# The last two chunks of a maxout layer in seven block products in place of eight

## The chip, the core and the metric

The kernel runs on one core of a Trainium2 chip. A core has TensorE (PE in the profile; its weight loads are PEld), VectorE (DVE), ScalarE (ACT), GpSimd (POOL) and SyncE (SP), whose queue starts most transfers (DMA). The measure is the device time of one execution in microseconds (us), as a median of runs.

## What is computed

```python
scores = scale * np.matmul(q, k.transpose(0, 1, 3, 2))      # 8 batches, 8 heads, 576 tokens, 64 wide
scores = np.where(mask, scores, -1000000000.0)              # mask: causal by blocks of 64 tokens
scores = scores - np.max(scores, axis=-1, keepdims=True)
attn = np.exp(scores)
attn = attn / (np.sum(attn, axis=-1, keepdims=True) + 1e-09)
attn_out = np.matmul(attn, v)
x = np.ascontiguousarray(attn_out.transpose(0, 2, 1, 3)).reshape(B * S, H * D)   # 4608 x 512
h = np.maximum(np.maximum(x @ w1, x @ w2), x @ w3)          # 512 x 768 each
out = h @ w_out                                             # 768 x 512
```

All is 32-bit. The weights come as 64-bit numbers and are rounded in the kernel.

## The kernel before

**Attention.** A `Pair` is two heads of one batch (four pairs a batch). `qk` makes the scores, `least` the row minima on VectorE, `exp` the exponentials on ScalarE, `turn` transposes them on VectorE into `pz`, `move` reshuffles `pz` into `pt` by eight transfers on SyncE's queue, and `pv` multiplies by the values. The result `x` is transposed: 128 features (one pair) by 512 tokens. The last 64 of a batch's 576 tokens (`ov`) are written to a scratch tensor `over` in device memory (method `put` of `Pair`; its end is the job `spilt`). TensorE runs `pv` of one pair with `qk` of the next (`both`); the last pair of all runs it by itself (`alone`).

**The layer.** A `Chunk` is 512 tokens of one batch; the ninth, `b == B`, is the leftover tokens of all batches, fetched back from `over`. Each 32-bit operand is split into two parts that TensorE takes at full rate: a high part (a cast on ScalarE: `xh`, `hh`) and a low part, the rest (a subtraction of two SBUF tensors on GpSimd or VectorE: `xl`, `hl`). A product of 128x128 by 128x512 is then three matmuls: high by high, high by low, low by high. The first layer (`product`) takes, for each of 6 blocks of 128 hidden units, 3 weight matrices and 4 blocks of features, three matmuls: 216 of them, each 512 columns wide, per chunk. `most` takes the running maximum: the first matrix is copied from PSUM on ScalarE, the other two are maxima on VectorE. The second layer (`project`) is 72 matmuls: for each of 4 token tiles 6 blocks, with `hh` and `hl` made in two groups of three blocks. `get` copies the result on ScalarE into `osb`, and `put` writes it out.

**Order.** Every step is a `Job` with a cost per engine, a rank, the jobs it waits for and the buffers it takes. `in_order` is run when the program is built: it fixes which engine takes a job (of those named in its cost) and the order on each engine. The chip then follows that order, engine by engine, and waits by semaphores on the data alone. PSUM has eight banks, five named `sb` (attention) and three named `pm` (layer). Ranks come from tables written by hand (`UNITS`, `PAIRS`, `STARTS`). The weights are prepared in the first 180 us and stay in SBUF as high and low parts (`wh`, `wl`, `woh`, `wol`).

Of the kernel before, what the change touches and what calls it, by code (L numbers as in the profile page):

```python
# [161 lines left out]
def kernel(  # L162
# [317 lines left out]
    class Head:  # L480
# [139 lines left out]
        def exp(self, eng, t):  # L620
            (nm, sm, _), c = self.stat, COL[t]
            self.p[t] = att.tile([P, P * (t + 1)], F32, name=f"p{t}", bufs=slots[f"p{t}"])
# [39 lines left out]
    class Pair:  # L662
# [124 lines left out]
        def plan4(self, first, tq, last):  # L787
# [307 lines left out]
    class Chunk:  # L1095


        def __init__(self, b, pairs, prior, start, end):
# [4 lines left out]
            xjobs = []
            for c in range(NC):
                if full:
                    ready = [pairs[c].ready]
                else:
                    ready = [job({"SP": LOAD}, start - 4, self.fetch, c, after=[q[c].spilt for q in pairs], take=("x32",), lasts=LOAD + DMA)]
# [202 lines left out]
```

## Time and profile before

| | |
|---|---|
| median of 3 runs | 879.0 us (878.9 to 883.0) |
| the profiled execution's own time | 879.9 us |
| its span, first to last instruction | 878.1 us |
| TensorE busy | 856.4 us, 98% |
| VectorE, ScalarE, GpSimd busy | 575.3, 463.7, 207.4 us |
| granted clock of TensorE, mean | 0.997 |

Times in rows are us from the start of the span. A timeline row gives start, duration, engine, line, operation, output and inputs, and in brackets the idle time ahead of it and what ended it. The profiled execution's own time is 1.8 us more than its span and 0.9 us more than the median.

### The profile page before, as it was taken

The page shows a single profiled execution, that of the slowest core. Times are in us where ns is not written, and L with a number is a line of the kernel's source. Part 1 is how long each engine was busy: PE and PEld are TensorE (multiplying, and loading weights), DVE is VectorE, ACT ScalarE, POOL GpSimd, SP SyncE. Part 2 cuts the span into 40 slices and gives each one's busy share as a digit, 9 for nine tenths or more (in the row PEclk, how much of TensorE's full clock was granted, in tenths as well). Part 3 has the DMA queues.
Part 4 walks back from the last instruction along what each step waited for, and adds up shares of the span by engine and source line. Part 5 has one row for each costly group of instructions (what it writes and reads, how often), then busy time and mean ns, then how long its engine had stood idle before and what let it go on. Part 6 is the DMA issues. An engine that isn't in the chain of part 4 may idle for free.

```text
span 878.1 us, 14264 instructions
## 1 busy us (share of the span) xinstructions
PE 856.4 (98%) x4646; PEld 661.7 (75%) x4646; DVE 575.3 (66%) x1583; ACT 463.7 (53%) x1269; POOL 207.4 (24%) x196
## 2 busy tenths in 40 slices
PE   7989999999999999999999999999999999999997
PEld 5656676777777777777777777777777778888885
DVE  5999998987877676857777677667666662222211
ACT  5778666765656454755576455645574343112102
POOL 1112442522415122422232223222241210001000
PEclk9999999999999999999999999999999999999999
DMA  6964365576565655565456555655566305001002
GB/s 156 239 192 107 90 148 155 117 170 137 129 139 124 153 112 106 106 147 115 109 119 149 115 117 116 159 110 118 118 162 133 83 22 147 1 1 49 1 0 49
DMA packets 233738, 99.26 MB, mean 113 GB/s; under 512 B 189888, under 2 KB 227776, under 8 KB 233664
## 3 DMA queue, kind: packets, MB, share of 16 engines
q1 hardware_dynamic: 219392, 95.99, 47.3%
q10 hardware_dynamic: 14272, 2.36, 1.5%
q8 instruction: 37, 0.61, 0.3%
q14 instruction: 37, 0.30, 0.1%
HBM read 41.94 MB, written 10.49 MB: 60 GB/s over the span
## 4 chain that ended last, share of the span: by engine, by line
PE 79%; DVE 11%; DMA 3%; ACT 2%; SPq 2%; issue 1%; POOL 1%; DVEq 0%; ACTq 0%; POOLq 0%
PE pm L1198 47%; PE pm L1232 14%; PE sb L1070 8%; PE sb L980 6%; PE sb L996 3%; DVE sb L460 3%; DMA nat<-in_k_dram 1%; DVE wo L361 1%; DVE pz L646 1%; DMA pt<-pz 1%; ACT p L626 1%; DMA wo<-in_moe_w_out_dram 1%; DVE wo L348 1%; SPq L656 1%; PE sb L580 1%
## 5 line engine op out<-in xcount | busy, mean ns | idle before, releaser
L1198 PE MATMUL pm<-xh,w 128*128 128x512 f32 x1296 | 424.4, 397 | 0.0
L1198 PEld LDWEIGHTS pm<-xh,w 128*128 128x128 f32 x1296 | 243.3, 188 | 55.3 <-issue 1.3
L1198 PE MATMUL pm<-xl,w 128*128 128x512 f32 x648 | 253.1, 391 | 0.5 <-POOL xl L273 0.5
L460 DVE CUSTOM_DVE_ANT_0 sb<-sb,mask 128x512 f32<-128x512 f32 (+3 forms) x288 | 144.8, 528 | 68.8 <-PE sb L980 42.7
L626 ACT ACTIVATE p<-sb,nm 128x256 f32<-128x256 f32 (+3 forms) x256 | 133.9, 530 | 63.7 <-DVE nm L460 60.0
L646 DVE STREAM_TRANSPOSE pz<-p 128x512 f32<-128x512 f32 (+1 forms) x280 | 137.9, 529 | 22.7 <-ACT p L476 18.0
L1198 PEld LDWEIGHTS pm<-xl,w 128*128 128x128 f32 x648 | 121.9, 188 | 25.2 <-POOL xl L273 0.9
L1211 DVE TENSOR_TENSOR m<-pm,m 128x512 f32<-128x512 f32 x108 | 73.3, 678 | 98.4 <-PE pm L1198 97.6
L1232 PE MATMUL pm<-wo,hh 128*128 128x512 f32 x432 | 135.2, 394 | 0.4 <-ACT hh L268 0.4
L478 POOL TENSOR_TENSOR p<-p,rs 128x128 f32<-128x128 f32 (+3 forms) x91 | 66.6, 754 | 236.6 <-DVE rs L785 220.4
L1070 PE MATMUL sb<-pt,vn 128*64 128x320 f32 (+2 forms) x840 | 90.7, 361 | 4.6 <-ACT p L626 2.1
L1232 PEld LDWEIGHTS pm<-wo,hh 128*128 128x128 f32 x432 | 79.9, 188 | 18.3 <-ACT hh L268 0.8
L268 ACT COPY m<-pm 128x512 f32<-128x512 f32 x54 | 31.6, 585 | 112.7 <-PE pm L1198 112.7
L1070 PEld LDWEIGHTS sb<-pt,vn 128*64 128x64 f32 x840 | 56.1, 137 | 42.4 <-issue 12.9
L1232 PE MATMUL pm<-wo,hl 128*128 128x512 f32 x216 | 84.4, 391 | 0.0
L980 PE MATMUL sb<-kq 64*128 64x512 f32 (+3 forms) x704 | 81.1, 354 | 1.9 <-ACT kq L268 0.5
L980 PEld LDWEIGHTS sb<-kq 64*128 64x128 f32 x704 | 58.1, 185 | 29.1 <-issue 13.7
L476 ACT ACTIVATE p<-p,rs 128x256 f32<-128x256 f32 (+3 forms) x133 | 66.8, 553 | 23.6 <-DVE rs L785 23.5
L273 POOL TENSOR_TENSOR kq<-nat,kq 128x1152 fp32r<-128x1152 f32 x21 | 56.4, 2684 | 71.8 <-ACT kq L268 39.8
L268 ACT CAST hh<-m 128x384 fp32r<-128x384 f32 x72 | 35.3, 514 | 49.6 <-PE pm L1232 28.0
L273 DVE TENSOR_TENSOR hl<-m,hh 128x384 fp32r<-128x384 f32 x54 | 39.3, 729 | 32.7 <-ACT hh L268 32.4
L273 POOL TENSOR_TENSOR xl<-x,xh 128x512 fp32r<-128x512 f32 x26 | 34.0, 1314 | 97.0 <-ACT xh L268 76.5
(105 smaller groups left out, 811.6 us busy)
## 6 DMA issues: line engine op xcount, KB each, us to landing
pt<-pz SPq DMA_DIRECT2D x224, 200.0 KB, 3.9
w<-in_moe_w_dram SPq DMA_DIRECT2D x18, 512.0 KB, 5.4
vn<-in_v_dram SPq DMA_DIRECT2D x64, 128.0 KB, 2.5
out_dram<-osb SPq DMA_DIRECT2D x32, 256.0 KB, 2.8
nat<-in_k_dram SPq DMA_DIRECT2D x112, 72.0 KB, 2.4
nat<-in_q_dram SPq DMA_DIRECT2D x96, 72.0 KB, 2.8
wo<-in_moe_w_out_dram SPq DMA_DIRECT2D x6, 512.0 KB, 5.9
nat<-in_q_dram ACTq DMA_DIRECT2D x16, 72.0 KB, 3.3
```

Of the source, the lines that this page charges most:

```text
L268: nc.scalar.copy(dst, src)
L273: {"DVE": nc.vector, "POOL": nc.gpsimd}[eng].tensor_tensor(out=dst, in0=a, in1=b, op=ALU.subtract)
L460: nc.vector.tensor_tensor_reduce(out=ps, in0=ps, in1=hidden, scale=-SCALE, scalar=first, op0=ALU.add, op1=ALU.min, accum_out=out_)
L476: nc.scalar.mul(p, p, r)
L478: nc.gpsimd.tensor_tensor(out=p, in0=p, in1=r.broadcast_to([P, p.shape[1]]), op=ALU.mult)
L626: nc.scalar.activation(dst, src, AF.Exp, bias=nm[:, c : c + 1], scale=-1.0, accum_out=sm[:, c : c + 1])
L646: nc.vector.transpose(dst, p[:, 0 : n * P])
L980: nc.tensor.matmul(ps, self.q[a][h.own, P * t : P * (t + 1)], self.k[b][h.own, 0:w], start=(a, b) == turns[0], stop=(a, b) == turns[-1],)
L1070: nc.tensor.matmul(o[h.own].rearrange("p (i u) -> p i u", u=n)[:, :, c0 : c0 + z - a], self.vn[:, kt, h.j, :], h.pt[:, :, a:z], start=(m = ...
L1198: nc.tensor.matmul(self.ps, w[i, f][:, c, :], xx, start=(c == 0 and s == 0), stop=(c == NC - 1 and s == 2))
L1211: nc.vector.tensor_tensor(out=m, in0=ps, in1=m, op=ALU.max)
L1232: nc.tensor.matmul(self.po, h, w[f], start=(f == 0 and s == 0), stop=(f == NF - 1 and s == 2))
```

## The change

The last batch's chunk and the chunk of leftovers, 1,024 tokens together, are taken as one by a new class `Double`. Its first layer is a 2x2 block product: two hidden blocks (`fp` numbers the three pairs of them) by two halves of the features on the weights' side, two halves of the features by two chunks on the data's side. Strassen's algorithm in Winograd's form makes it from seven block products, `P1` to `P7`, of 6 matmuls each. There are 9 such sets (3 pairs of blocks, 3 matrices), numbered `n`. For each set the sums of weight blocks `S1` to `S4` are made anew: two additions that put high and low part together (512 wide), four block sums, and four splits into high and low (all 256 wide). The sums of data blocks `T1` to `T4` are made once, in place, before the first set; the leftovers are fetched for that into buffers of the attention that have come free (`nat`, `vn`, `p4`). The results are put together from PSUM with temporaries `t0`, `t1`, `t2` (`p1`, `U2`, `p5`, `U3`, `C11` to `C22`), and `M12`, `M21`, `M22` are the running maxima. In a set, `P2` is added to `P1`'s bank and `P3` to `P5`'s, after a copy of each on ScalarE. The second layer follows for all 8 token tiles. The attention's and the weights' tables are changed too.

```diff
+    LAST = 2
...
-    UNITS = (0, 0, -1, 0, -4, 1, 0, 4, 9, 2, -8, 2, 2, 7, -3, -2, -2, -2, 0, -3, -2, -7, -5, -7)
-    PAIRS = (-1, 17, 1, 0, 4, 0, 0, -1, -8, -13, -15, -23)
-    STARTS = (0, 1, -2, -2, -2, -3, -2, -21, -1, -4, -1)
+    UNITS = (0, 0, -1, 0, -4, 1, 0, 0, 9, 2, -8, 2, 1, 7, -3, -2, -2, -1, 0, -6, -3, -7, -7, -9)
+    PAIRS = (-1, 17, 1, 0, 4, 0, 0, -1, -8, -13, -15, -23, 0, 2, -4, -1, 0, 0, 0, 0, 0, 0, 0, 0, 0, -4, -2, -2, -6, -8, -4, -6)
+    STARTS = (7, 2, -2, -2, -2, -3, -3, -22, -4, -5, 3)
...
+    SEVEN = {
+        "P1": ("A11", "B11", "a"),
+        "P2": ("A12", "B21", "a"),
+        "P3": ("S4", "B22", "c"),
+        "P4": ("A22", "T4", "e"),
+        "P5": ("S1", "T1", "c"),
+        "P6": ("S2", "T2", "b"),
+        "P7": ("S3", "T3", "d"),
+    }
+    FIRST_SEVEN = ("P1", "P5", "P2", "P6", "P7", "P3", "P4")
+    NEXT_SEVEN = ("P1", "P6", "P2", "P5", "P7", "P3", "P4")
...
+    class Double:
...
+            for c in range(2):
...
+                    for k, hp in (("x1", c), ("x3", c + 2))
+                )
+                b11, b21 = (pairs[c + n].ready for n in (0, 2))
...
+                l11 = parts("B11", "x0", b11)
+                t1 = sub("x1", "x0", "x0", l11, b12)
+                l1 = parts("T1", "x0", t1)
+                l22 = parts("B22", "x3", b22)
+                t3 = sub("x3", "x1", "x1", t1, b22)
+                l3 = parts("T3", "x1", t3)
+                t2 = sub("x3", "x0", "x0", l1, b22)
+                l2 = parts("T2", "x0", t2)
+                l21 = parts("B21", "x2", b21)
+                t4 = sub("x0", "x2", "x2", t2, l21)
+                l4 = parts("T4", "x2", t4)
...
+            hold = job({"SP": 1.0}, start, lambda eng: None, after=(prior.projected,), take=("hi", "hi"))
...
+            fresh = dict.fromkeys(("S1", "S2"), [hold]) | dict.fromkeys(("S3", "S4"), [last.last4, *free["p2"]])
...
+            for fp in range(3):
+                for i in range(3):
+                    left = self.lefts(n, fp, i, start + step * 7 * n, [*split, *(gone if n == 3 else ())], fresh)
+                    split = [left[x][0] for x in left]
+                    done, ranks = {}, {}
+                    for k, name in enumerate(NEXT_SEVEN if n else FIRST_SEVEN):
+                        a, b, bank = SEVEN[name]
+                        first = name in ("P1", "P6", "P5", "P7", "P4")
+                        after = [chain, ops[b, 0], ops[b, 1], prior.projected]
...
+                        chain = done[name] = job(
+                            {"PE": 6 * pe(N)}, start + step * (7 * n + k), self.product, n, fp, i, name, after=after, take=(TAGS[bank],) if first else ()
+                        )
...
+                        vec, both, m0 = {"DVE": dve(N) + 5.0}, two(N), i == 0
+                        if name == "P1":
+                            ev("p1", {"ACT": act(N)}, chain, ends.get("t0"), gate)
+                        if name == "P6":
+                            ev("U2", vec, chain, done["p1"], give=("sb",))
...
+                            ev("U3", vec, chain, done["U2"], ends.get("t1"), gate, give=("sb",))
+                            ev("C22", both, done["U3"], done["p5"])
...
+                        if name == "P3":
+                            ev("C12", vec, chain, done["U2"], done["U3"], give=("sb",))
...
+                        if name == "P4":
+                            ev("C21", vec, chain, done["C22"], give=("pm",))
...
+        def lefts(self, n, fp, i, rank, free, fresh):
+            two = lambda n: {"POOL": pool(n), "DVE": dve(n) + 5.0}
+            r = rank - 12
+            w = [
+                job(two(512), r, self.whole, n, fp, i, j, after=[units[i, 2 * fp + j].done, *free], ports=True) for j in range(2)
...
+            s1 = job(two(256), r, self.part, n, "S1", after=w[1:], ports=True)
+            s3 = job(two(256), r, self.part, n, "S3", after=[*w, s1], ports=True)
+            s2 = job(two(256), r, self.part, n, "S2", after=[s1, s3], ports=True)
+            s4 = job(two(256), r, self.part, n, "S4", after=[s2], ports=True)
+            out_ = {}
+            for name, after in (("S2", [s2, s4]), ("S1", [s1, s2]), ("S3", [s3]), ("S4", [s4])):
+                h = job({"ACT": act(256, False)}, r, self.high_s, n, name, after=[*after, *fresh[name]])
+                out_[name] = [job(two(256), r, self.low_s, n, name, after=(h,), ports=True)]
...
+        def product(self, eng, n, fp, i, name):
+            a, b, bank = SEVEN[name]
+            first = name not in ("P2", "P3")
+            if first:
+                pool_ = psm if TAGS[bank] == "pm" else psa
+                self.ps[bank] = pool_.tile([P, N], F32, name=TAGS[bank])
+                self.ps[n, bank] = self.ps[bank]
+            ps = self.ps[n, bank]
+            ah, al = self.left(n, fp, i, a)
+            for c in range(2):
+                bh, bl = (self.op(b, c, low) for low in (0, 1))
+                for s, (w, xx) in enumerate(((ah, bh), (ah, bl), (al, bh))):
+                    nc.tensor.matmul(ps, w[:, c, :], xx, start=(first and c == 0 and s == 0), stop=(c == 1 and s == 2), **({} if first else dict(skip_group_check=True)))
...
-    made[-1].alone(rank + SECOND)
+    made[-1].alone(rank + LAST)
...
-    for b in range(B + 1):
-        prior = Chunk(b, pairs[b] if b < B else pairs, prior, starts[b], starts[b + 1])
+    for b in range(B - 1):
+        prior = Chunk(b, pairs[b], prior, starts[b], starts[b + 1])
+    Double(pairs[B - 1], pairs, prior, starts[B - 1], starts[B + 1])
```

How the order moves, at three places. First TensorE at the last attention output (`L1070` and `L1072` are `pv`, `L1232` and `L1226` the second layer of batch 6's chunk, `L1198` a product of the last batch's chunk). Before:

```order
L1232 MATMUL pm<-wo_1815,hh 128x512 x2
L1232 MATMUL pm<-wo_1815,hl 128x512
L1198 MATMUL pm<-xh_7811,w_340 128x512
L1198 MATMUL pm<-xl_7819,w_340 128x512
L1198 MATMUL pm<-xh_7811,w_340 128x512
L1070 MATMUL sb<-pt,vn_103 64x320 x6
L1070 MATMUL sb<-pt,vn_103 64x4x48 x2
L1070 MATMUL sb<-pt,vn_103 64x4x16 x2
L1070 MATMUL sb<-pt,vn_103 64x256 x2
L1070 MATMUL sb<-pt,vn_103 64x4x32 x2
L1198 MATMUL pm<-xh_7814,w_340 128x512
```

TensorE after the change, at the same `pv`:

```order
L1226 MATMUL pm<-wo_1601,hh 128x512 x2
L1226 MATMUL pm<-wo_1601,hl 128x512
L1072 MATMUL sb<-pt,vn_103 64x320 x6
L1072 MATMUL sb<-pt,vn_103 64x4x48 x2
L1072 MATMUL sb<-pt,vn_103 64x4x16 x2
L1226 MATMUL pm<-wo_1618,hh 128x512 x2
L1226 MATMUL pm<-wo_1618,hl 128x512
...
L1226 MATMUL pm<-wo_1601,hl 128x512
L1072 MATMUL sb<-pt,vn_103 64x256 x2
L1072 MATMUL sb<-pt,vn_103 64x4x32 x2
L1226 MATMUL pm<-wo_1618,hh 128x512 x2
```

The `pv` now comes after 9 matmuls of the second layer and not after all 72, and its two halves stand apart, with 18 matmuls between them; 45 follow the second half, then the first `P1`.

Second, SyncE's queue at the last moves (`L656` and `L657` are `move`, `L1245` and `L1237` write results out, `L1187` and `L1414` fetch leftovers, `L897` and `L899` write them to scratch). Before:

```order
L1187 DMA x_7901<-over_116 128x512
L656 DMA pt<-pz 128x1x400 x4
L1245 DMA out_dram<-osb 128x512
L656 DMA pt<-pz 128x1x400 x4
L1245 DMA out_dram<-osb 128x512 x2
L897 DMA over_117<-ov 128x64
L1187 DMA x_8021<-over_117 128x512
```

SyncE's queue after the change:

```order
L899 DMA over_116<-ov 128x64
L657 DMA pt<-pz 128x1x400 x8
L1414 DMA nat<-over_116 128x512
L899 DMA over_117<-ov 128x64
L1237 DMA out_dram<-osb 128x512
L1414 DMA p_7937<-over_117 128x512
L1237 DMA out_dram<-osb 128x512 x3
```

All eight moves now stand together, with no write of results between them, and the fetches of the last leftovers go to `nat` and to `p4`'s buffer.

Third, ScalarE where batch 6's second layer ends and the last chunk's first layer begins (`osb` is `get`; `hh` is a high part). Before:

```order
L268 CAST hh<-m 128x384
L268 COPY osb<-pm 128x512
L268 COPY m<-pm 128x512
L268 COPY osb<-pm 128x512
L268 COPY m<-pm 128x512 x2
L268 CAST hh<-m 128x384 x3
```

ScalarE after the change, at the same end of batch 6's second layer (`p_8048` and `xh_8054` are high parts of `T3` and `T2`, `p_8016` of `S3`, the next `hh` of `S1`, `vn_103` is the copy of `P1`, then `hh` of `S2` and `q8r` of `S4`):

```order
L269 CAST hh<-m 128x384
L269 CAST pz<-x_7776 128x512
L269 COPY osb<-pm 128x512 x2
L269 CAST p_8048<-vn_102 128x512
L269 CAST xh_8054<-x_7533 128x512
L269 CAST p_8016<-m 128x256
L269 CAST hh<-m 128x256
L269 COPY vn_103<-pm 128x512
L269 CAST hh<-m 128x256
L269 CAST q8r_100<-m 128x256
```

Behind the last copy of the second layer ScalarE now has four high parts to make before `P1`'s copy; before, only a copy of the next chunk's first product stood there.

## Rows read from the trace of the kernel before

**Rows 1.** The page: busy time of TensorE, and the ending chain by line.
```profile
PE 856.4 (98%) x4646; PEld 661.7 (75%) x4646; DVE 575.3 (66%) x1583; ACT 463.7 (53%) x1269; POOL 207.4 (24%) x196
...
PE pm L1198 47%; PE pm L1232 14%; PE sb L1070 8%; PE sb L980 6%; PE sb L996 3%; DVE sb L460 3%; DMA nat<-in_k_dram 1%; DVE wo L361 1%; DVE pz L646 1%; DMA pt<-pz 1%; ACT p L626 1%; DMA wo<-in_moe_w_out_dram 1%; DVE wo L348 1%; SPq L656 1%; PE sb L580 1%
```

**Rows 2.** Busy by stretch: length, PE, PEld, DVE, ACT, POOL, clock, DMA share, GB/s.
```profile
738.00:858.00 120.00, 119.97 (x544) 98.99 (x542) 24.81 (x36) 18.80 (x35) 5.62 (x5) 1.00 0.05 15
```

**Rows 3.** Timeline of VectorE, 747 to 790 us: running maxima (start, us, ...).
```profile
747.56 0.69 DVE L1211 TENSOR_TENSOR m<-pm,m 128x512 f32<-128x512 f32 x1 [3.63 <-PE pm L1198]
...
788.36 0.69 DVE L1211 TENSOR_TENSOR m<-pm,m 128x512 f32<-128x512 f32 x1 [4.82 <-PE pm L1198]
```

**Rows 4.** Timeline of TensorE after the last `qk` and at the last `pv`.
```profile
723.85 0.74 PE L1232 MATMUL pm<-wo,hh 128*128 128x512 f32 x2
...
738.31 0.39 PE L1198 MATMUL pm<-xh,w 128*128 128x512 f32 x1
...
739.11 3.03 PE L1070 MATMUL sb<-pt,vn 128*64 128x320 f32 x28
```

**Rows 5.** Timeline of TensorE, then ScalarE, in the last projection, 857 us to the end.
```profile
858.71 0.73 PE L1232 MATMUL pm<-wo,hh 128*128 128x512 f32 x2 [0.42 <-ACT hh L268]
859.30 0.50 PE L1232 MATMUL pm<-wo,hl 128*128 128x512 f32 x1
...
873.03 0.39 PE L1232 MATMUL pm<-wo,hl 128*128 128x512 f32 x1
...
873.50 0.59 ACT L268 COPY osb<-pm 128x512 f32<-128x512 f32 x1 [3.49 <-PE pm L1232]
```

**Rows 6.** The tile pt, 725 to 745 us: its transfers.
```profile
L656 SPq DMA_DIRECT2D pt<-pz x8: 549/804/1065, 728.0 to 734.5; - x8
...
DMA to landing us min/median/max: 3.3/3.9/4.5
```

**Rows 7.** Timeline of the SyncE queue, 725 to 745 us.
```profile
727.98 3.11 SPq L656 DMA_DIRECT2D pt<-pz  x4
731.19 0.55 SPq L1245 DMA_DIRECT2D out_dram<-osb  x1
```

**Rows 8.** Timeline of ScalarE, 272 to 273 us.
```profile
272.03 0.62 ACT L268 CAST xh<-x 128x512 fp32r<-128x512 f32 x1
272.54 0.52 ACT L268 CAST hh<-m 128x384 fp32r<-128x384 f32 x1
```

**Rows 9.** Timeline of GpSimd at three places where VectorE works too.
```profile
768.26 1.01 POOL L273 TENSOR_TENSOR hl<-m,hh 128x384 fp32r<-128x384 f32 x1 [40.65 <-ACT hh L268]
...
789.72 2.60 POOL L273 TENSOR_TENSOR xl<-x,xh 128x512 fp32r<-128x512 f32 x2 [20.45 <-issue]
...
693.63 1.00 POOL L478 TENSOR_TENSOR p<-p,rs 128x256 f32<-128x256 f32 x1 [7.33 <-ACT hh L268]
694.59 1.33 POOL L273 TENSOR_TENSOR hl<-m,hh 128x384 fp32r<-128x384 f32 x1
```

**Rows 10.** Timeline of VectorE at the same places.
```profile
767.80 0.56 DVE L273 TENSOR_TENSOR hl<-m,hh 128x384 fp32r<-128x384 f32 x1 [0.58 <-ACT hh L268]
768.63 1.06 DVE L273 TENSOR_TENSOR hl<-m,hh 128x384 fp32r<-128x384 f32 x1 [0.27 <-ACT hh L268]
...
791.01 0.69 DVE L1211 TENSOR_TENSOR m<-pm,m 128x512 f32<-128x512 f32 x1 [1.96 <-PE pm L1198]
...
693.59 1.45 DVE L273 TENSOR_TENSOR hl<-m,hh 128x384 fp32r<-128x384 f32 x2
```

**Rows 11.** Timeline of TensorE, 289 to 291 us.
```profile
290.07 1.30 PE L1070 MATMUL sb<-pt,vn 128*64 128x320 f32 x8 [0.88 <-DMA pt<-pz]
```

More of the change, by code (lines that the diff above doesn't have):

```diff
@@ L621, in exp @@
             (nm, sm, _), c = self.stat, COL[t]
[L622 removed]
+            self.p[t] = att.tile([P, P * (4 if t == 2 else t + 1)], F32, name=f"p{t}", bufs=slots[f"p{t}"])[:, 0 : P * (t + 1)]
             dst, src = self.p[t], self.ps.pop(t)
@@ L810, in plan4 @@
             join((last,), ("q8",))
+            self.last4 = last
             return last
@@ L1098, in __init__ @@
         def __init__(self, b, pairs, prior, start, end):
-            self.b, self.pairs, self.hs, self.his, self.los = b, pairs, {}, {}, {}
+            self.b, self.pairs, self.hs, self.his, self.los, self.lows = b, pairs, {}, {}, {}, []
             step = (end - start) / (4 * NF * NC)
             self.x, self.xh, self.xl = [None] * NC, [None] * NC, [None] * NC
-            full = b < B
             xjobs = []
             for c in range(NC):
[L1105 to L1108, printed above, removed]
+                ready = [pairs[c].ready]
                 h = job({"ACT": act(N, False)}, start - 2, self.x_high, c, after=ready, take=(f"xh{c}",))
@@ L1162, in __init__ @@
                     l = job({"POOL": pool(n), "DVE": dve(n) + 5.0}, r, self.low, tt, fs, after=(h,), ports=True)
+                    self.lows.append(l)
                     for f in fs:
@@ L1179, in x_high @@
         def x_high(self, eng, c):
-            if self.b < B:
-                self.x[c] = self.pairs[c].x
+            self.x[c] = self.pairs[c].x
             self.xh[c] = xp.tile([P, N], F32R, name=f"xh{c}", bufs=1)
             copy(eng, self.xh[c], self.x[c])
-        def fetch(self, eng, c):
-            self.x[c] = xp.tile([P, N], F32, name="x32", bufs=slots["x32"])
-            nc.sync.dma_start(self.x[c], overs[c])
         def x_low(self, eng, c):
@@ L1241, in put @@
         def put(self, eng, tt):
-            ob = self.hs.pop(("ob", tt))
-            if self.b < B:
-                r0 = self.b * S + P * (0, 1, 3, 2)[tt]
+            r0 = self.b * S + P * (0, 1, 3, 2)[tt]
+            nc.sync.dma_start(out[r0 : r0 + P, :], self.hs.pop(("ob", tt)))
+    SEVEN = {
[7 more added lines that the diff above has]
+    }
@@ new lines @@
+    FIRST_SEVEN = ("P1", "P5", "P2", "P6", "P7", "P3", "P4")
+    NEXT_SEVEN = ("P1", "P6", "P2", "P5", "P7", "P3", "P4")
+    TAGS = {"a": "pm", "b": "sb", "c": "sb", "d": "sb", "e": "pm"}
+    HOMES = {}
+    for operand, own in (
+        ("B11", ("xh0", "xl0", "xh1", "xl1")),
+        ("T1", ("kq.0", "kq.0", "kq.1", "kq.1")),
+        ("T2", ("xh2", "xl2", "xh3", "xl3")),
+        ("T3", ("p3.0", "p3.1", "p2.0", "p2.1")),
+        ("B22", ("pz.0", "pz.0", "pz.0", "pz.1")),
+        ("B21", ("pt.0", "pt.0", "pt.0", "pt.1")),
+        ("T4", ("pz.1", "pz.1", "pt.1", "pt.1")),
+    ):
+        for place, tag in enumerate(own):
+            HOMES[operand, place // 2, place % 2] = tag, sum(h[0] == tag for h in HOMES.values())
```

225 lines of the change are left out of this document (224 added, 1 removed).

## Prediction

> **What bounds the kernel now.** I read the page first. TensorE is busy 98% of the span, and the chain that ended last is mostly TensorE: 47% in the first layer's products, 14% in the second layer [rows 1]. A share over the whole span does not say what the changed stage is worth, so the second view is the stretch after the attention, 738 to 858 us. There TensorE is busy 119.97 of 120 us at a granted clock of 1.00, its higher level, while VectorE is busy 24.81, ScalarE 18.80 and GpSimd 5.62 us [rows 2]. So in this stage the end is set by the number of matmuls times their distance, and three other engines have room for new work.
>
> The distance comes from VectorE's running maxima. A hidden block has 36 matmuls, 12 for each weight matrix; the maxima at 747.56 and 788.36 follow the second matrix of blocks that are five apart, so 180 matmuls took 40.80 us, **0.2267 us per matmul** [rows 3]. As a check I build the old end from it: first product of the last batch's chunk at 738.31, the last `pv` for 3.03 us [rows 4], and 432 + 144 matmuls of two first and two second layers, the last of which then starts at 738.31 + 3.03 + 575 x 0.2267 = 871.7. It did start at 873.03 [rows 5]. So the old stage has 1.3 us of waits (0.42 at 858.71 is one), and the rest is matmuls. From the last start to the span's end it is 5.1 us: the last copy on ScalarE [rows 5] and the write, which the change leaves alone.
>
> **Removed.** Nine sets of 42 are 378 matmuls in place of 432: 54 x 0.2267 = 12.2 us. With the old waits gone as well the last matmul starts at 738.31 + 3.03 + 521 x 0.2267 = 859.5, and the span ends at **864.5**. To this the new waits are added.
>
> **Added: the last `pv`.** Call T the end of the last `qk`, 723.85 before [rows 4]. Before, 66 matmuls (15.0 us) lay between it and `pv`; now 48 products and 9 of the second layer do, 12.9 us. What `pv` needs is the last of the eight moves. It started at 734.5 and a move lands in 3.3 to 4.5 us, 3.9 in the middle [rows 6]. The order takes the write of results from between the moves (0.55 us of issue [rows 7] and its gap, 0.7 together), so the last move starts at T + 9.9 and lands at T + 13.8. TensorE comes at T + 12.9 and waits **0.9 us** (0.3 to 1.5 by the landing times). Behind it stand 63 matmuls of the second layer, then `P1`, and all of them shift.
>
> **Added: `P5` of the first set.** Its weights `S1` come from ScalarE, whose queue is in order. With P as the start of `P1`, the last copy of batch 6's second layer starts at about P + 0.25 and takes 0.59 [rows 5]. Then come two casts of 512 (0.51 from start to start [rows 8]) and two of 256 (half of it, 0.27 each, my estimate). `S1` is ready at about P + 2.4, and `P5` could start after the six matmuls of `P1`, at P + 1.36: 1.05 us late. Its third matmul needs the low part as well, on GpSimd. GpSimd took 1.01 us for 384 columns and 1.30 for 512 [rows 9], so 256 cost about 0.72, my estimate. That is ready at P + 3.2, or 0.6 later if VectorE is in the way, against a need at P + 2.9. Together with slower first matmuls after a pause (0.50 in place of 0.39 at 859.30 [rows 5]) I take **1.9 us** (1.1 to 2.6).
>
> **Added: work beside the nine sets.** A set is 42 x 0.2267 = 9.52 us, nine are 85.7. By the order GpSimd gets 12 operations of 512 and 51 of 256: 12 x 1.30 + 51 x 0.72 = 52 us. VectorE gets 42 operations on PSUM at 0.69 [rows 10], 29 us, and 54 that read two SBUF tensors, 33 of 512 and 21 of 256. One of those of 384 columns cost 0.42 behind another (below), so 0.56 and 0.28 by width, my estimate: 24 us. Neither engine is full by itself. But the two hinder each other. A subtraction of 384 on VectorE takes 0.56 alone; the one at 768.63 took 1.06, since GpSimd worked on SBUF from 768.26 to 769.27, and 769.27 + 0.42 is its end [rows 9, 10]. A maximum that reads PSUM beside a busy GpSimd stayed at 0.69 (791.01) [rows 10]. So 52 + 24 = 76 of 85.7 us are wanted of something that only one of the two has at a time. Who gets it next is seen at 693.59: VectorE's two subtractions took 1.45 together, and GpSimd's second operation 1.33 in place of 1.01 [rows 9, 10]. They took turns, one operation each. A VectorE operation thus loses at most 1.3 us at a time, and the order leaves more than that: `M12`, which the next set's `P1` copy waits for, has from `P4`'s start to `P2`'s start of the next set, 3 x 1.36 = 4.1 us, for a `C12` of 0.69, its own 0.56 and a copy of 0.59: 2.2 us spare. The weight sums are made a set ahead, save that set 1's come barely in time for its `P6`. I take **0.3 us** in all (0 to 4, that is up to 0.5 a set).
>
> The Trainium skill, "SBUF — State Buffer", section "SBUF: two separate sides", calls the pair of ports that VectorE and GpSimd share an exclusive lock held for a whole instruction, for which the loser fully blocks. The 1.06 us agree. It lets whichever starts first have it, which alone would let GpSimd's runs win each time; that is the last rival below.
>
> **Moved.** The tables alter the attention's order from about 290 us on. There one `pv` waited 0.88 us for its moves [rows 11]; three products, 0.68 us, now stand ahead of it. I take **-0.5 us** (-0.7 to 0).
>
> **At no cost.** The splits and differences of the data, some 14 casts, 14 low parts and 8 differences, lie beside the 72 matmuls of batch 6's second layer (16.3 us) and the first set; a cast is 0.51, a low part 1.30 or less. If that cover failed, `P6` and `P7` of the first set would wait for `T2` and `T3`, about 1.3 us for each operation late. The last leftovers' fetch lands about 5 us before its need. The weights' casts for later sets (four of 256 a set, 1.1 us) have ScalarE nearly to themselves.
>
> **Sum.** 864.5 + 0.9 + 1.9 + 0.3 - 0.5 = 867.1 us of span, against 878.1. The profiled execution's time is 1.8 more than its span and 0.9 more than the median of 879.0, so the median should be 867.1 + 0.9 = **868.0 us**. All low bounds give 866.0, all high ones 873.5.
>
> **Rivals.**
>
> *Small waits in each set.* VectorE's queue is in order: an operation held up by GpSimd also holds the PSUM operations behind it, and with them a bank or a copy that TensorE needs. For it: 76 of 85.7 us wanted; against it: the 2.2 us spare. At 0.4 to 0.8 us in each of eight sets the time is 871 to 874.
>
> *VectorE becomes the bound, no change.* If each of its 54 two-input operations waited a whole GpSimd operation (52/63 = 0.83 us), VectorE would need 29 + 24 + 45 = 98 us for 85.7: 12.4 us more, 880.4. Against it: GpSimd is busy only 61% of the time, and a wait begins somewhere inside its operation.
>
> *Slower: GpSimd keeps its turn through a run.* The order puts two sums and four parts in a row on it, 2 x 1.30 + 4 x 0.72 = 5.5 us. If `M12` had to wait for all of it, `P2` would be 5.5 - 2.2 = 3.3 us late in seven of the sets: +23 us, 891. It decides from 2.2 us a set (15.4/7). Against it: the turns at 693.59.
>
> **How the numbers follow.** About 0.5%, 4.4 us, is what a measurement of this kernel can tell from no change: faster ends at 874.6, slower begins at 883.4. The forecast's case (865 to 870.9) has 0.66, since the removed matmuls are certain and their price is that of this very stage; the small waits 0.20; VectorE as the bound or high ends of several terms at once (874.6 to 883.4) 0.08; GpSimd's runs 0.06. Faster is 0.66 + 0.20 = 0.86, same 0.08, slower 0.06. The range takes the forecast's case and most of the small waits: 865.0 to 873.5.
>
> **What would show it.** Right: 378 matmuls of the new products at 0.227 us; a wait of 1 to 2.6 us ahead of `P5` in the first set, ended by ScalarE or GpSimd; 0.3 to 1.5 us at the last `pv`, ended by the moves; VectorE's operations on two SBUF tensors longer by up to 1.3 us each, those on PSUM not; no other pause of TensorE above 0.5 us in the sets; 5.1 us from the last matmul to the end. Wrong: a pause in each set ahead of `P2` (late copy, behind `M12`), ahead of `P6` or `P5` (late sums) or for a bank; or a granted clock below 1.00 after 738 us, by which every matmul would cost more.

## The result

The changed kernel took **869.5 us**, median of 4 runs (867.9 to 869.8), beside 879.1 for the kernel before: ratio 0.988 (0.985 to 0.991). In a later, longer comparison it was 870.8 beside 878.6, ratio 0.991 (0.988 to 0.993). So it is 8 to 10 us faster, where 11 were forecast. Its profiled execution has a span of 866.1 us, against 878.1.

The page of the kernel after, busy time [rows 1].

```profile
PE 845.7 (98%) x4592; PEld 649.6 (75%) x4592; DVE 647.5 (75%) x1678; ACT 488.2 (56%) x1342; POOL 279.8 (32%) x260
```

TensorE has 54 matmuls fewer and 10.7 us less work, and still is busy 98% of the span. Busy time by stretch, with the columns of [rows 2], for the nine sets and then the second layer:

```profile
738.00:828.60 90.60, 88.85 (x381) 70.76 (x380) 72.56 (x102) 28.77 (x65) 61.18 (x62) 1.00 0.01 4
828.60:862.00 33.40, 32.83 (x145) 26.84 (x143) 10.82 (x32) 12.29 (x36) 0.00 (x0) 1.00 0.19 55
```

In 90.6 us of sets TensorE is busy 88.85. VectorE went from 24.81 us in a stretch of 120 to 72.56 in one of 90.6, and GpSimd from 5.62 to 61.18. The timeline of TensorE shows where it waited. The rows are every pause after 738 us that it lists (it leaves out those of 0.15 us and less), the first matmul of the sets (738.46), the first of the second layer (828.63) and the last of all. Under them stands ScalarE's last copy [rows 4, 5].

```profile
738.46 0.39 PE L1507 MATMUL pm<-xh,w 128*128 128x512 f32 x1
...
740.99 0.74 PE L1507 MATMUL sb<-kq,hh 128*128 128x512 f32 x2 [1.01 <-ACT hh L269]
742.17 0.50 PE L1507 MATMUL sb<-kq,hl 128*128 128x512 f32 x1 [0.45 <-POOL hl L274]
...
763.29 1.67 PE L1507 MATMUL pm<-pt,w 128*128 128x512 f32 x6 [0.28 <-ACT vn L269]
...
828.63 0.62 PE L1581 MATMUL pm<-wo,hh 128*128 128x512 f32 x2
...
861.04 0.39 PE L1581 MATMUL pm<-wo,hl 128*128 128x512 f32 x1
...
861.51 0.59 ACT L269 COPY osb<-pm 128x512 f32<-128x512 f32 x1 [3.49 <-PE pm L1581]
```

The pauses are where the prediction had them, at `P5` of the first set: 1.01 us for `S1`'s high part, 0.45 for its low part. One of 0.28 us at 763.29 had no place of its own in the sum: `P2` of the third set waits for the copy of `P1` (`vn` is `t0`). From the last matmul's start to the end it is 5.1 us, as before.

ScalarE's timeline ahead of that first `P5`:

```profile
738.70 0.59 ACT L269 COPY osb<-pm 128x512 f32<-128x512 f32 x1 [3.54 <-PE pm L1226]
739.18 0.62 ACT L269 CAST p<-vn 128x512 fp32r<-128x512 f32 x1
739.71 0.62 ACT L269 CAST xh<-x 128x512 fp32r<-128x512 f32 x1
740.22 0.41 ACT L269 CAST p<-m 128x256 fp32r<-128x256 f32 x1
740.53 0.40 ACT L269 CAST hh<-m 128x256 fp32r<-128x256 f32 x1
```

And GpSimd's:

```profile
737.09 4.16 POOL L1480 TENSOR_TENSOR m<-m 128x256 f32<-128x256 f32 x4
741.21 0.91 POOL L274 TENSOR_TENSOR hl<-m,hh 128x256 fp32r<-128x256 f32 x1
```

ScalarE works without a gap from 738.70 on: copy, the casts of `T3` and `T2`, then `S3` and `S1` (the `hh` at 740.53). A cast of 256 columns took 0.31 us from start to start (0.27 forecast). GpSimd's four block sums took 4.16 us, 1.04 each where 0.72 was forecast, and `S1`'s low part starts only behind the last of them, at 741.21, though its high part is done at 740.93. Busy time in the 10.5 us ahead of the sets and in set 0:

```profile
728.00:738.46 10.46, 10.46 (x50) 8.55 (x46) 10.10 (x7) 4.56 (x9) 9.92 (x8) 1.00 0.20 74
738.46:750.30 11.84, 10.38 (x43) 7.64 (x42) 9.86 (x12) 5.85 (x14) 10.98 (x10) 1.00 0.07 24
```

VectorE and GpSimd are nearly full in both. ScalarE is not (5.85 of 11.84 us); there it is the order of its queue that makes `S1` wait.

The lengths of the nine sets, from the first matmul of one `P1` to that of the next (the last: to the second layer), read from TensorE's timelines of the runs:

```
                 set 0   set 1   set 2   set 3   sets 4, 5  set 6   sets 7, 8
after            11.84    9.82   10.24    9.81   9.63 9.62   9.96   9.62 9.63
e10_same         11.90    9.84   10.21    9.83   9.63 9.63   9.92   9.63 9.63
e5_sums_once     11.91    9.63    9.93    9.63   9.63 9.62   9.63   9.63 9.62
e6_sums_twice    13.26   10.89   10.19   13.54   9.63 9.63  10.90  10.04 9.63
e7_all_twice     12.03   13.97   10.15   17.34  11.35 9.63  16.19  11.29 9.63
e3_eight         13.21   11.03   11.24   11.23  11.03 11.02 11.06  11.03 11.03
```

An undisturbed set is 9.63 us, not 42 x 0.2267 = 9.52. The difference stands in its second part: in set 4 the 18 matmuls of `P1`, `P6` and `P2` take 4.08 us (780.17 to 784.25), 0.2267 each, and the 24 of `P5`, `P7`, `P3` and `P4` take 5.55 (to 789.80), 0.231 each.

### The profile page after: what moved, and what is told of

It is laid out like the page before. It is cut to its first block, busy times and chain, and to the rows that moved or that the text cites. A ratio compares the mean times of both kernels' runs of the same rounds, so it can differ in the third digit from the quotient of the medians.

```text
span 866.1 us, 14491 instructions
## 1 busy us (share of the span) xinstructions
PE 845.7 (98%) x4592; PEld 649.6 (75%) x4592; DVE 647.5 (75%) x1678; ACT 488.2 (56%) x1342; POOL 279.8 (32%) x260
## 4 chain that ended last, share of the span: by engine, by line
PE 80%; DVE 9%; DMA 3%; ACT 3%; issue 2%; POOL 2%; SPq 1%; ACTq 0%; DVEq 0%; POOLq 0%
PE pm L1192 37%; PE pm L1226 10%; PE sb L1072 8%; PE sb L982 7%; PE sb L1507 5%; PE pm L1507 4%; PE pm L1581 4%; PE sb L998 3%; DVE sb L461 2%; ACT p L627 1%; SPq L657 1%; DMA pt<-pz 1%; DVE wo L362 1%; PE sb L581 1%; DVE pz L647 1%
## 5 line engine op out<-in xcount | busy, mean ns | idle before, releaser
L1192 PE MATMUL pm<-xh,w 128*128 128x512 f32 x1008 | 336.0, 399 | 0.0
L1192 PEld LDWEIGHTS pm<-xh,w 128*128 128x128 f32 x1008 | 189.3, 188 | 44.3 <-issue 1.2
L1192 PE MATMUL pm<-xl,w 128*128 128x512 f32 x504 | 197.0, 391 | 0.5 <-POOL xl L274 0.5
L479 POOL TENSOR_TENSOR p<-p,rs 128x384 f32<-128x384 f32 (+3 forms) x88 | 65.4, 767 | 214.1 <-DVE rs L786 197.2
L1192 PEld LDWEIGHTS pm<-xl,w 128*128 128x128 f32 x504 | 94.8, 188 | 19.1 <-POOL xl L274 0.9
L1226 PE MATMUL pm<-wo,hh 128*128 128x512 f32 x336 | 105.4, 395 | 0.0
L1072 PE MATMUL sb<-pt,vn 128*64 128x320 f32 (+2 forms) x840 | 90.8, 361 | 1.7 <-ACT p L627 0.7
L1072 PEld LDWEIGHTS sb<-pt,vn 128*64 128x64 f32 x840 | 55.1, 137 | 40.6 <-issue 9.8
L1226 PEld LDWEIGHTS pm<-wo,hh 128*128 128x128 f32 x336 | 62.0, 188 | 13.8 <-issue 0.3
L1226 PE MATMUL pm<-wo,hl 128*128 128x512 f32 x168 | 65.6, 390 | 0.0
L274 DVE TENSOR_TENSOR hl<-m,hh 128x384 fp32r<-128x384 f32 (+1 forms) x51 | 39.4, 772 | 26.8 <-ACT hh L269 26.6
L269 ACT CAST kq<-nat 128x1152 fp32r<-128x1152 f32 x24 | 27.8, 1157 | 42.9 <-PE sb L982 37.5
L627 ACT ACTIVATION_READ_ACCUMULATOR p<-sb,nm 128x1 f32 x256 | 51.6, 202 | 0.0
L269 ACT CAST hh<-m 128x384 fp32r<-128x384 f32 (+1 forms) x70 | 34.0, 505 | 27.9 <-DVE m L1205 12.5
```

What stands on the lines that cost most here:

```text
L269: nc.scalar.copy(dst, src)
L274: {"DVE": nc.vector, "POOL": nc.gpsimd}[eng].tensor_tensor(out=dst, in0=a, in1=b, op=ALU.subtract)
L479: nc.gpsimd.tensor_tensor(out=p, in0=p, in1=r.broadcast_to([P, p.shape[1]]), op=ALU.mult)
L627: nc.scalar.activation(dst, src, AF.Exp, bias=nm[:, c : c + 1], scale=-1.0, accum_out=sm[:, c : c + 1])
L1072: nc.tensor.matmul(o[h.own].rearrange("p (i u) -> p i u", u=n)[:, :, c0 : c0 + z - a], self.vn[:, kt, h.j, :], h.pt[:, :, a:z], start=(m = ...
L1192: nc.tensor.matmul(self.ps, w[i, f][:, c, :], xx, start=(c == 0 and s == 0), stop=(c == NC - 1 and s == 2))
```

## The experiments

The theory under test is that of the prediction: in this stage the time is the number of matmuls times their distance, plus a few short pauses; the other engines' work is hidden as long as their operations take turns. The rivals are that the tables carry the gain, that the sets are partly bound by VectorE and GpSimd, and that GpSimd's runs hold VectorE up.

**Eight products' time with all of the new work.** The six matmuls of `P7` are issued twice in each set.

```diff
-            for c in range(2):
+            for again in range(2 if name == "P7" else 1):
+                for c in range(2):
...
```

> The changed kernel with the six matmuls of P7 issued twice in each set (the second pass starts its bank anew, so the values stay): eight products' time on TensorE with all the work that seven products need on the other engines. Theory: the stage is TensorE's, 54 x 0.2267 = 12.2 us come back less up to 0.5 us of pauses that the longer set hides: 881.2 to 881.7 us, 1.5 to 3 us slower than the kernel before. Rival: the sets are partly bound by VectorE and GpSimd, then the added matmuls fill pauses and cost 8 us or less: below 877.5.

Measured: **881.3 us** beside 878.4 (ratio 1.003, 1.002 to 1.005). An undisturbed set is 11.03 us in place of 9.63, and from the first `P1` to the last matmul it took 134.29 in place of 122.58, 11.7 us more: nine times 1.40, less 0.9 of pauses that the longer sets hide. The gain is the matmuls, and without their saving the change costs 3 us.

**The tables apart.** First the sets with the old tables, then the old chunks with the new tables.

```diff
-    LAST = 2
+    LAST = 9
...
-    STARTS = (7, 2, -2, -2, -2, -3, -3, -22, -4, -5, 3)
+    STARTS = (0, 1, -2, -2, -2, -3, -2, -21, -1, -4, -1)
```

> The nine sets of seven products with the old tables UNITS, PAIRS and STARTS and the old place of the last pv (LAST 9). Theory: nearly all of the gain is the 54 matmuls that are gone (12.2 us, and 1.3 us of old waits, less 3.4 us of new pauses in the sets), and the tables give what the pauses of TensorE before 300 us show: 0.89 to 0.17, 0.71 to 0.48 and 0.88 to 0, 1.8 us. So 871.3 us (870.3 to 872.5), still 7 to 9 us under the kernel before. Rival: the new tables are what lets the sets be fed in time, and without them the first set waits several us more for its data sums: 874 or more.

Measured: **872.2 us** beside 878.4 (0.993, 0.991 to 0.995). Two of TensorE's pauses in its timeline, in the attention and in the first set:

```profile
290.52 1.80 PE L1072 MATMUL sb<-pt,vn 128*64 128x320 f32 x13 [1.50 <-DMA pt<-pz]
...
749.41 0.74 PE L1507 MATMUL pm<-pt,w 128*128 128x512 f32 x2 [1.34 <-POOL pt L274]
```

The wait for the moves at 290 us is back at 1.50 [rows 11]; none of the ten other profiled executions, all with the new tables, has one there. The sets do not suffer: from the first `P1` to the last matmul 122.32 us, against 122.58. They have the same shortage in another place: the pause ahead of `P5` is gone and one of 1.34 stands in `P2`, ahead of its low part of `B21` (`pt`). The rival that the new tables feed the sets is out, and so is the one that they carry the gain: without them 6 us of it are left.

> The kernel before, with its two chunks in eight products, under the new tables (UNITS, PAIRS, STARTS, and the last pv at 2 in place of 9). Theory: the tables are worth the 1.8 us of pauses that went before 300 us, so 877.3 us (876.5 to 879). Rival: the tables are worth 4 us or more by themselves, 875 or less, and the seven products give the smaller part. Other rival: they only fit the new end, and the old end waits under them: above 880.

The edit is the reverse: the new numbers and the last `pv` at 2 in the kernel before. Measured: **878.2 us** beside 878.4 (0.999, 0.998 to 1.001). Alone the tables are worth 1.8 us at most, and perhaps nothing.

**`S1` sooner.** Its parts go to `S3`'s buffers and the reverse, and in the first set it goes ahead.

```diff
-            for name, after in (("S2", [s2, s4]), ("S1", [s1, s2]), ("S3", [s3]), ("S4", [s4])):
-                h = job({"ACT": act(256, False)}, r, self.high_s, n, name, after=[*after, *fresh[name]])
+            for name, after in (("S2", [s2, s4]), ("S1", [s1] if n == 0 else [s1, s2]), ("S3", [s3]), ("S4", [s4])):
+                early = 20 if (n, name) == (0, "S1") else 0
+                h = job({"ACT": act(256, False)}, r - early, self.high_s, n, name, after=[*after, *fresh[name]])
...
-                    self.s = {name: (hi + lo)[2 * k : 2 * k + 2] for k, name in enumerate(("S2", "S1", "S3", "S4"))}
+                    self.s = {name: (hi + lo)[2 * k : 2 * k + 2] for k, name in enumerate(("S2", "S3", "S1", "S4"))}
```

> The changed kernel with the first set's S1 made earlier: its two parts go to the buffers of S3 (free since the attention's end) and S3's to those of hh and hl, S1's high part waits for its own sum alone and, in the first set, stands ahead of T2's cast on ScalarE and of the later sums on GpSimd. Theory: the two pauses ahead of P5 (1.01 and 0.45 us, with slower restarts about 2 us) shrink to 0.5 or less and nothing else needs S1's place: 867.7 to 868.5 us against 869.5, TensorE idle ahead of the first P5 below 0.3 us. Rival: what is late is the whole queue of sums, so the pause moves to P6 or P7 of the first set (S2, T2, S3 or T3) and the time stays within 0.5 us of 869.5.

Measured: **869.9 us** beside 878.4 (0.991, 0.988 to 0.993): no change against 869.5. TensorE's pauses in the first two sets:

```profile
740.03 0.73 PE L1508 MATMUL sb<-kq,p 128*128 128x512 f32 x2 [0.19 <-ACT p L269]
741.04 1.20 PE L1508 MATMUL sb<-kq,p 128*128 128x512 f32 x4 [0.28 <-POOL p L274]
...
743.91 0.73 PE L1508 MATMUL pm<-pt,w 128*128 128x512 f32 x2 [0.74 <-DVE pt L274]
...
752.86 0.50 PE L1508 MATMUL sb<-xh,hl 128*128 128x512 f32 x1 [0.79 <-DVE hl L274]
```

Ahead of `P5` 0.19 and 0.28 us are left, as the theory had it, but 0.74 now stands in `P2` (`B21`'s low part, on VectorE) and 0.79 in the second set's `P6` (`S2`'s low part). The rival was right in kind: the pause moves, though it named `P6` and `P7` of the first set.

**All first operands by need.** On top of that, by ranks alone: `B21` and `T2` earlier, `T3` last.

```diff
+                    r = start - 2 - {"B21": 18, "T2": 12}.get(key, 0)
...
+                    r = start - 2 - (16 if (a, to) == ("x3", "x0") else 0)
```

> The changed kernel with the first set's operands made in the order in which its products need them: S1 as in the earlier run (in S3's buffers, ahead of the later sums), then B21, T2's difference and parts and S2, and T3 last, by ranks alone. Theory: what is late at the first sets is the order in VectorE's, GpSimd's and ScalarE's queues, with room in them for all that the first two sets need; then the pauses after 738 us fall from 1.7 us (2.3 with S1 alone moved) to below 1.0, and the time is 868 to 869 beside 869.5. Rival: all three engines together are short of time just here, about 8 us of work for two sets' operands, so the pause only changes its place: 869 to 871.

Measured: **870.3 us** beside 878.6 (0.990, 0.988 to 0.992). The pauses are 0.66, 0.42 and 0.98 us, 2.06 in all against 1.74 in the changed kernel, at `P5`, `P6` and the next `P6`. So the time is in the range of the rival. VectorE and GpSimd are short of time together here (rows above), and neither order that was tried helps; that no other one would is not shown.

**Without the sums.**

```diff
+            if n in (0, 3):
...
+                s1 = job(two(256), r, self.part, n, "S1", after=w[1:], ports=True)
...
+                self.first = s1, s2, s3, s4
+            s1, s2, s3, s4 = self.first
```

> Leaves out the weight sums of seven of the nine sets: the two whole additions and four block sums are made for sets 0 and 3 only, and the other sets split what stands there (casts and low parts stay). Theory: the sums cost TensorE only the few pauses that it has after the first set (0.28 us ahead of a P2 and about 0.4 us of lost starts ahead of it), so 868.8 us (868 to 869.5); VectorE's maxima of two SBUF tensors (M12, M21, M22), 1.05 to 1.14 us now, fall below 0.8. Rival: the sharing of GpSimd's and VectorE's work costs several us in losses too small to show as pauses: 866.5 or less.

Measured: **868.3 us** beside 879.6 (0.987, 0.984 to 0.990). Seven of the last eight sets are now at 9.63 us or less, and from the first `P1` to the last matmul it is 121.65 us, 0.9 less. So the sums of these seven sets cost TensorE about 1 us; the casts and low parts, and the sums of the other two sets, stay. The two slowest groups of maxima fell less than I expected, to 0.89 and 0.96 us, while a third went to 0.69; the low parts on GpSimd are still beside them.

**More work for GpSimd.** Its whole additions after the first set twice; then its low parts twice as well.

```diff
+            for again in range(2 if eng == "POOL" and n > 0 else 1):
+                {"DVE": nc.vector, "POOL": nc.gpsimd}[eng].tensor_tensor(out=dst, in0=a, in1=b, op=ALU.add)
...
+            for again in range(2 if eng == "POOL" and n > 0 else 1):
+                minus(eng, self.s[name][1], t, self.s[name][0].bitcast(F32))
```

> Each whole addition that GpSimd makes after the first set is made twice (11 more operations of 512 columns, the result the same): GpSimd's runs of sums grow from about 5.5 to 8.5 us. Theory: VectorE and GpSimd take turns, an operation of VectorE waits for one of GpSimd and not for the run; GpSimd is busy 61 + 11 x 1.6 = 79 of 88 us, and what shows is sums late for some sets: 870 to 874 us. Rival: GpSimd keeps its turn through the run, P1's copy comes behind M12 by 3 us more in seven sets: 885 or more.

Measured: **876.7 us** beside 879.6 (0.996, 0.994 to 0.998), 2.7 us over the range that I gave. The profiled execution is the fastest of its ten, with 873.3 us. TensorE's pauses in its sets up to 775 us:

```profile
738.93 0.73 PE L1508 MATMUL sb<-kq,hh 128*128 128x512 f32 x2 [1.01 <-ACT hh L269]
740.14 0.50 PE L1508 MATMUL sb<-kq,hl 128*128 128x512 f32 x1 [0.48 <-POOL hl L274]
...
752.59 0.50 PE L1508 MATMUL sb<-xh,hl 128*128 128x512 f32 x1 [0.68 <-DVE hl L274]
...
763.69 1.66 PE L1508 MATMUL pm<-pt,w 128*128 128x512 f32 x6 [0.27 <-ACT vn L269]
...
774.72 0.50 PE L1508 MATMUL sb<-xh,hl 128*128 128x512 f32 x1 [1.97 <-POOL hl L274]
```

Busy time and clock behind two of them (columns as in [rows 2]):

```profile
740.00:744.00 4.00, 3.86 (x11) 3.06 (x12) 3.77 (x4) 0.59 (x1) 3.49 (x4) 0.64 0.02 4
...
776.00:780.00 4.00, 4.00 (x13) 3.12 (x13) 3.35 (x5) 0.59 (x1) 2.95 (x3) 0.67 0.02 4
```

GpSimd's run of four whole additions took 6.04 us (762.37), and still the wait for `P1`'s copy in the third set is 0.27 us, as it was with half the run. The rival, 3 us more at that place in seven sets, is out. The turns can be seen as well, in a maximum of VectorE that lies wholly within GpSimd's run:

```profile
762.37 6.04 POOL L1466 TENSOR_TENSOR x<-w 128x512 f32<-128x512 f32 x4
...
763.59 1.06 DVE L1531 TENSOR_TENSOR m<-osb,m 128x512 f32<-128x512 f32 x1
```

What is late is the sums themselves (`hl` at 774.72, 1.97 us; another 0.98 at 806.48). The rest is the clock: after the pauses at 740 and at 775 us it shows 0.64 and 0.67 in a stretch of 4 us, which the theory had not counted.

> As the kernel with the whole additions twice, and GpSimd's low parts of the weight sums after the first set twice too (21 more of 256 columns). Theory: GpSimd now needs 61 + 17 + 21 x 0.9 = 97 us for a stage of 88 and becomes the bound: 877 to 882 us, TensorE idle ahead of P6 or P5 in most sets. Rival: there is more room than that, since its operations take 1.0 and 0.72 us less when VectorE does not stand in the way: below 873.

Measured: **890.5 us** beside 879.6 (1.012, 1.010 to 1.015). GpSimd as the bound was right in the main, the time was 8.5 us over the range. The two longest pauses of set 3 in TensorE's timeline:

```profile
781.67 0.80 PE L1509 MATMUL sb<-xh,hh 128*128 128x512 f32 x1 [3.00 <-ACT hh L269]
...
785.01 0.79 PE L1509 MATMUL sb<-xh,hl 128*128 128x512 f32 x1 [2.11 <-POOL hl L274]
```

Busy time from the first `P1` to the second layer:

```profile
741.00:852.60 111.60, 95.16 (x380) 73.62 (x379) 74.00 (x102) 28.58 (x65) 94.18 (x93) 0.94 0.01 3
```

GpSimd's work there is 94.18 us, not more than the 97 forecast. But it does not run without gaps (twice it waits 1.5 us for a cast on ScalarE), and it ends at 845.2, with 7 us of products still to come. Sets 1, 3 and 6 are 4.3, 7.7 and 6.6 us longer than undisturbed ones. From the first `P1` to the last matmul it is 143.99 us, 21.4 more than in the changed kernel. The granted clock of the stretch is 0.94 and not 1.00, so at most 111.6 x 0.06 = 6.7 us of these are the clock's (in a part of its low stretches TensorE stood idle anyway), and pauses of 14.8 us after the first set are most of the others. The rival's condition is not met: no whole addition of GpSimd took less than 1.28 us, no block sum or low part less than 0.72, so that much less is in no row.

**VectorE alone.**

```diff
-    two = lambda n: {"POOL": pool(n), "DVE": dve(n) + 5.0}
+    two = lambda n: {"DVE": dve(n) + 5.0}
```

> All sums and low parts of the weights on VectorE, none on GpSimd, which gets more of the data's low parts in exchange. Theory: without GpSimd beside it VectorE takes its operations at 0.69 us from PSUM and about 0.6 and 0.35 for 512 and 256 columns of two SBUF tensors: 29 + 45 x 0.6 + 72 x 0.35 = 81 of 86 us, just room enough, but its queue is in order and the waits for PSUM stand in it: 870 to 875 us. Rival: the other engine's hindrance was worth nothing and one engine cannot do it in time: above 876.

Measured: **878.8 us** beside 879.6 (1.000, 0.998 to 1.002); the time is the rival's, its reason holds only in part. In sets 1 to 5 one engine was enough: they are at 9.63 to 9.84 us, with VectorE busy 46.48 of 49.54 us (756.46 to 806.00). The later three have pauses of 0.5 to 0.7 us that VectorE ends, and two of them took in matmuls of the second layer. What it lost stands at the ends: set 0 takes 15.78 us, 3.9 more than in the changed kernel, and the stretch from set 6 to the last matmul 6.2 more. In set 0 `P5`'s third matmul waits 2.71 us for `S1`'s low part on VectorE, the clock falls to 0.61 in the next 4 us, and a second pause of 1.78 us comes with the second layer. TensorE's timeline at these places:

```profile
746.93 0.50 PE L1507 MATMUL sb<-kq,hl 128*128 128x512 f32 x1 [2.71 <-DVE hl L274]
...
748.14 2.76 PE L1507 MATMUL pm<-pt,w 128*128 128x512 f32 x6
...
841.98 0.74 PE L1581 MATMUL pm<-wo,hh 128*128 128x512 f32 x2 [1.78 <-ACT hh L269]
```

And busy time and clock behind the first of them:

```profile
748.00:752.00 4.00, 4.00 (x12) 3.09 (x12) 3.54 (x6) 1.48 (x3) 0.69 (x1) 0.61 0.01 4
```

This run also gives VectorE's prices with GpSimd out of the way. Its groups by form, 745 to 828 us (count, busy us, mean ns):

```profile
L1480 DVE TENSOR_TENSOR x<-x 128x256 f32<-128x256 f32 x12 | 5.1, 424 | 0.3
...
L1530 DVE TENSOR_TENSOR w<-osb,w 128x512 f32<-128x512 f32 x5 | 3.5, 692 | 0.2
L1530 DVE TENSOR_TENSOR m<-vn,m 128x512 f32<-128x512 f32 x4 | 2.8, 692 | 0.1
```

Groups of the changed kernel (`osb<-sb,vn` reads PSUM, the other three of VectorE are maxima of two SBUF tensors), and GpSimd's whole additions:

```profile
L1530 DVE TENSOR_TENSOR osb<-sb,vn 128x512 f32<-128x512 f32 x9 | 6.2, 690 | 3.3 <-PE sb L1507 3.1
L1530 DVE TENSOR_TENSOR w<-osb,w 128x512 f32<-128x512 f32 x7 | 6.0, 860 | 0.2
...
L1530 DVE TENSOR_TENSOR m<-osb,m 128x512 f32<-128x512 f32 x4 | 4.4, 1088 | 0.1
L1530 DVE TENSOR_TENSOR m<-vn,m 128x512 f32<-128x512 f32 x4 | 4.2, 1048 | 0.1
...
L1465 POOL TENSOR_TENSOR x<-w 128x512 f32<-128x512 f32 x8 | 13.4, 1684 | 0.4
```

A maximum of two SBUF tensors takes 0.692 us with GpSimd idle and 0.86 to 1.09 beside it, in the mean of a group; an operation that reads PSUM takes 0.69 beside it too. GpSimd's own whole additions take 1.68 us beside VectorE, where 1.30 was forecast from [rows 9]. Single operations lose more than the mean: the longest of VectorE in set 0, a difference of 512 columns, took 1.67 us. So the two hinder each other, at times for as much as a whole operation, as the Trainium skill says of the shared port pair ("SBUF — State Buffer", section "SBUF: two separate sides").

**The changed kernel again.**

> The changed kernel as it is, once more beside the kernel before on one chip, for a narrower interval: 869.5 us, 9 to 11 us under the kernel before, and pauses of TensorE ahead of the first P5 (1.0 and 0.45 us) as in the first profile; what changes from run to run should lie before 250 us, where it waits for transfers.

Measured: **870.8 us** beside 878.6 (0.991, 0.988 to 0.993), 7.8 us less, a little under the 9 to 11 expected. The pauses at `P5` are 1.01 and 0.53 us, the later one 0.29: the sets repeat to 0.1 us. Its profiled span is 869.1 us, 3.0 more than the first one's, and the difference arises before 250 us. Busy time and clock (the third number from the end) in two early stretches of the first execution:

```profile
16.00:18.00 2.00, 2.00 (x20) 2.00 (x19) 1.21 (x5) 1.82 (x5) 0.00 (x0) 1.00 0.74 239
...
62.00:64.00 2.00, 1.84 (x10) 1.80 (x10) 1.86 (x9) 1.70 (x5) 0.00 (x0) 0.63 1.05 354
```

One of them in this execution, two pauses of TensorE after it, and VectorE ahead of the second pause:

```profile
16.00:18.00 2.00, 2.00 (x12) 2.00 (x11) 0.72 (x3) 0.97 (x3) 0.00 (x0) 0.50 0.60 197
...
183.63 2.89 PE L1072 MATMUL sb<-pt,vn 128*64 128x320 f32 x26 [0.97 <-DMA pt<-pz]
193.42 1.55 PE L982 MATMUL sb<-kq 64*128 64x512 f32 x16 [1.60 <-POOL kq L274]
...
188.05 1.38 DVE L951 STREAM_TRANSPOSE nat<-nat 128x1152 f32<-128x1152 f32 x1 [3.39 <-DMA nat<-in_q_dram]
```

Both start the same row of matmuls at 15.3 us. In the first execution the clock is at 1.00 there, in the second at the lower level, 0.50, and the same later matmul starts at 34.24 in one and at 37.09 in the other. But the first has its stretch at the lower level too, at 62 to 66 us, and by 167 us only 0.9 us of the lead are left. The rest of the difference are waits for transfers: at 183.63 the second waits 0.97 us for the moves, where the first waits 0.17, and at 193.42 it waits 1.60 for a tile that the first has in time; the input of that tile came late, VectorE waited 3.39 us for it and 0.46 in the first. So the expectation, transfers before 250 us, holds for most of it.

## Why the prediction was right, and where it was off

**The base.** 54 matmuls at 0.2267 us: shown from both sides, by the seven products and by giving the six matmuls back (11.7 of 12.2). The second layer runs as forecast: from 828.63 to 861.04 us, 32.41 for 143 distances of 0.2267 = 32.42.

**The first set** was put at 1.9 us and cost 11.84 - 9.63 = 2.2. The mechanism (two pauses, ScalarE then GpSimd) is that of the trace. That VectorE and GpSimd are nearly full there, so that neither reordering tried saves it, I had not said. The cover that the prediction put at no cost did hold: no pause stands at `P6` or `P7` of the first set. But VectorE was busy 10.10 and GpSimd 9.92 of the 10.46 us ahead of it.

**The work beside the sets** is the term that was mis-sized: 0.3 us, and it was 2.3. Of these 1.3 are waits in sets 1, 2, 3 and 6 with the slower starts behind them (78.33 us for sets 1 to 8, less 8 x 9.63). Only the one of 0.28 us is long enough to be listed. The weight sums account for about 0.9 of them. The other 1.0 is the distance of the matmuls, 9.63 for 9.52 us a set, also with the sums left out. It stands in `P5`, `P7`, `P3` and `P4` of every undisturbed set, and with all sums on VectorE, or `S1` in another buffer, too; so neither GpSimd's work nor that buffer makes it. The cause stays open. From `P1`'s start to the last matmul I had 118.1 + 1.9 + 0.3 = 120.3 us, and it took 122.6.

**The spare of the copy.** The prediction gave `M12` 2.2 us to spare, with 0.56 us for it. `M12` and the copy behind it in the third set:

```profile
761.50 1.07 DVE L1530 TENSOR_TENSOR m<-vn,m 128x512 f32<-128x512 f32 x1
...
762.65 0.59 ACT L269 COPY vn<-pm 128x512 f32<-128x512 f32 x1 [3.46 <-DVE m L1530]
```

It took 1.07, VectorE had other operations ahead of it, and the spare was used up: the copy starts when `M12` ends, and `P2` 0.28 us late. The 0.56 was too low even for VectorE alone, where 512 columns take 0.69 us and 256 take 0.42; at these the 54 operations come to about 32 us and not 24. GpSimd's part was too low as well: its 63 operations were put at 52 us and took 64.

**The last `pv`** was put at 0.9 us; it waited 0.36 in the first profile (its first half took 3.39 us there and 2.79 in the second, so 0.6 us in all), and no pause stands there in the second, nor in the seven other executions with this order. The moves [rows 6], and TensorE's pause:

```profile
L657 SPq DMA_DIRECT2D pt<-pz x8: 543/670/1315, 710.2 to 716.1; - x8
...
DMA to landing us min/median/max: 3.2/4.7/5.0
...
720.78 1.56 PE L1072 MATMUL sb<-pt,vn 128*64 128x320 f32 x10 [0.36 <-DMA pt<-pz]
```

They stand in one row as the order said, the last starts at 716.1, and the median landing is 4.7 us where 3.9 were taken. That the wait nearly vanishes and that [rows 11]'s pause is gone makes this side better than the +0.4 us of the sum, by how much can't be told from single executions, which differ by 3 us here: the sum has the first `P1` at 741.7, and it came at 738.46 and 741.38.

**The rivals.** Small waits in each set came true in kind and not in size: 1.3 us over eight sets. GpSimd did not keep its turn, and neither engine became the bound; doubling GpSimd's additions and low parts shows that the second limit is near (890 us). The forecast of 868.0 was 1.5 to 2.8 us low. From the first `P1` on the sum was 2.3 us low, mostly by the sets, and ahead of it it seems to have been a little high. That the two errors partly cancel is luck. (All low bounds add up to 866.1, not 866.0.)

## What to carry to other kernels

A stage in which one engine is busy all the time gives back the removed instructions at their distance, nearly in full, as long as the engines that take over the work have room; add up their operations with the price that they have beside each other (here 0.86 to 1.09 us, not 0.69), and not their price alone. Then look at the first few microseconds of the stage by themselves, since operands for several steps are wanted there at once: that was the largest new wait, and each of the two reorderings only moved the wait.

## What was not expected of the hardware

A pause of TensorE can cost more than itself. With VectorE alone, after 2.71 us of waiting (on top of 1.29), the clock fell to its lower level, and six matmuls took 2.76 us where they take 1.52. Shorter pauses can be followed by this too, and need not be. Six executions have the same two pauses at the first `P5`, 1.01 us and 0.42 to 0.63. Behind them the clock was 1.00 in five; in the one with the whole additions twice it fell (0.64 in 4 us), and its set 0 was 13.26 us long, where the changed kernel's was 11.84.

One execution of the same kernel can be 3 us longer than another. Of the two profiled here one had the lower clock at 16 us and the other at 62, which left a difference of 0.9 us; transfers that came later at 180 to 193 us made most of the rest.
